# Output stores of a fused attention and feed-forward kernel: from SyncE's queue to ScalarE's, with a new plan of the order

## The chip, the cores and the metric

The kernel runs on one core of one Trainium2 chip. The metric is the device time in microseconds of one execution. TensorE (PE), VectorE (DVE), ScalarE (ACT) and GpSimd (POOL) compute; SyncE (SP) only issues DMAs. ACT and POOL have queues of their own in which DMAs can be issued too.

## The reference

Eight batches of eight heads, 576 queries each, head size 64. The keys of a batch are 16 beacons, which every query sees, and 576 causal keys. The outputs of all heads make a matrix x of 4608 tokens by 512, which goes through a gated feed-forward layer of width 1536. Cut to what matters:

```python
k_all = np.concatenate([beacon_k, k], axis=2)          # (8, 8, 592, 64)
v_all = np.concatenate([beacon_v, v], axis=2)
scores = np.matmul(q, k_all.transpose(0, 1, 3, 2)) / np.sqrt(64)
scores = np.where(causal, -1e9, scores)                # beacons never masked
a = np.exp(scores - scores.max(-1, keepdims=True))
a /= a.sum(-1, keepdims=True) + 1e-09
attn = np.matmul(a, v_all)                             # (8, 8, 576, 64)
x = attn.transpose(0, 2, 1, 3).reshape(4608, 512)
out = (np.maximum(x @ w_gate, 0) * (x @ w_val)) @ w_out
```

Inputs and the output are float32; the matmuls run in bfloat16.

## The kernel before

**Stages.** For every batch q, k and v are loaded in pieces of 128 partitions by 512 elements into eight staging tiles `st` (the helper `staged`, loads at L557 to L657), rounded to bfloat16 tiles `h` or `v` (L518, L471, mostly on POOL), and q and k are turned by TensorE against an identity (L529) and copied out of PSUM into `qT` and `kT` (the helper `copy`, L467 on ACT, L469 on DVE). In batch 7 the turning is done by a DMA transpose (L574). Scores are made in steps of 64 by 64 tiles (L756) into PSUM banks; DVE adds the mask and finds the row's extreme (L704), ACT takes the exponential with its sum (L711), DVE the reciprocal (L717), POOL multiplies the probabilities by it (L722). A DMA transpose issued by SP turns the probabilities, `pb` to `pTb` (L842; in the first batch TensorE does it, L832). The products with v (L852, L875) are copied into `xT`, the feed-forward input, which holds all tokens transposed.

**Feed-forward.** The function `ffn` works on ten spans of tokens (`SPANS`, 240 to 512 wide). For each of 12 slices of the width there are four gate matmuls (L913), a relu out of PSUM by ACT into a tile `g` (L924), four value matmuls (L918), and a product by DVE into `hT` (L929). Then, for every 128 tokens of the span, 12 output matmuls (L944) fill a PSUM bank; ACT or DVE copies it into one of three tiles `osb` (L954), and a DMA stores it (L958). The feed-forward work of early tokens runs between the attention work of later batches. All its PSUM comes from a share of at most three banks (`F_MOST`); scores have at most five (`SC_MOST`), out of eight in all.

**What sets the order.** The order is not written by hand. Every piece of work is a task given to `Plan.add` with its engine (or several to choose from), a cost, what it depends on, the buffers that it holds, and a priority. `Plan.order` (L190) then makes a list schedule: at each step it takes the task that can start first, then by lateness and priority, and books its cost on its engine. SP's queue is one such engine, called DMA; tasks of DMA carry a pair, the time for the issue and the time on the wire. The order that comes out is what each engine's queue gets, and engines work through their queues strictly in that order. While TensorE has nothing to do in the plan's first 160 us, filler matmuls (L996) are put in.

**Names that the change touches.** `BEHIND` (L44) makes the load at a place in a batch's list wait until a quad of another batch has been normalised, by a small memset on POOL that holds the staging tile. `W0` (L55) is the time in the plan before which no weight load (`weight`, L479, issued by POOL at L481) is placed. `PACE` (L66) times the batch number (and a half for its second quad) is the time before which no scores of it are placed (L978). A store is one task of DMA (L961) behind its copy (L960):

```python
q_ = nc.scalar if c else nc.sync
ev = add("ACT" if c else ("ACT", "DVE"), {"ACT": c_act(w), "DVE": c_dve(w)}, evict, (prev,), (ps[c], osb[c]), -1000 + prio)
add("DMA", (0.4, 0.78 / halves), store, (ev,), (osb[c],), prio + OUT)
```

`c` is 1 only for the second half of the very last 64 tokens, which are split in two columns of 256; that one store is issued by ACT, the other 37 by SP.

Of the kernel before, what the change touches and what calls it, by code (L numbers as in the profile page):

```python
# [20 lines left out]
RANK1 = -14.0  # L21
# [12 lines left out]
NEXT = -0.5  # L34
ON_PE = 2
TURN = (7,)
TURN_FIRST = 100
TURN_LOAD = 1.5
BIGSTEP = 2
# [1 line left out]
ENG = [("POOL", "DVE"), ("POOL",), ("POOL",)]  # L41
F_MOST = 3
HELD = {(1, 0): ("v", 0, 0), (1, 2): ("g", 0, 1024), (1, 4): ("v", 0, 1024)}
BEHIND = {(2, 2): (1, 0), (2, 7): (1, 1)}  # L44
MARK = 0.08
AB_FIRST = 0
W_FIRST = 0
# [4 lines left out]
ORDER0 = ("k00", "q00", "K", "Q", "k10", "q10", "v", "v", "k01", "q01", "k11", "q11", "v", "v", "v")  # L52
W_COLS = [(0, 512), (512, 512), (1024, 512)]
W_ROWS = 4
W0 = 14.0  # L55
W_STEP = 1.4
W_ISSUE = 0.85
W_MOVE = 0.72
# [4 lines left out]
SPANS = [240, 336, 512, 512, 512, 512, 512, 512, 512, 448]  # L63
FIRST_MOST = 3
AFTER = [[0.0, 12.0]]
PACE = 38.0  # L66


class Slots:
# [227 lines left out]
def kernel(  # L297
# [99 lines left out]
    def c_act(n):  # L397
        return 0.06 + 0.00083 * n
# [98 lines left out]
    def new_batch(b, prio, work):  # L497
# [54 lines left out]
        def load_pair(kind, p, prio):  # L552

            src, s0 = {"k": (k, 0), "q": (q, 64 - Nb)}[kind]
            st = staged()

            def fetch(_):  # L557
                if b in TURN:
                    for i in range(2):
                        nc.sync.dma_start(st.tile.rearrange("p (n h d) -> p h n d", h=2, d=D)[:, i],  # L560
                                          src[b, 4 * (p // 2) + p % 2 + 2 * i, s0:s0 + MAIN, :].rearrange("(n p) d -> p n d", p=P))
                    return
                nc.sync.dma_start(st.tile.rearrange("p (h e) -> p h e", h=2),
                                  src[b, bass.ds(4 * (p // 2) + p % 2, 2, step=2), s0:s0 + MAIN, :].rearrange("h (p j) d -> p h (j d)", j=4))

            ld = add("DMA", (1.0, TURN_LOAD) if b in TURN else (0.5, 0.87), fetch, (held,), (st,), prio[0])
            dst = t.kT if kind == "k" else t.q
            h16, ca = rounded(dst, st, P, neg_scale if kind == "q" else 1.0, prio, ld,
                              lambda to, src: [(to, src)] if b in TURN else [(
                to.rearrange("p (j h d) -> p h j d", h=2, j=4), src.rearrange("p (h j d) -> p h j d", h=2, j=4))])  # L570
            zeros = on_zeros.get(b) if kind == "q" else None
            c0 = Nb if kind == "k" else 64
            if b in TURN:
                t.rows[kind, p] = [add("DMA", (1.22, 0.177 * 4), lambda _: nc.sync.dma_start_transpose(  # L574
                    dst.tile[:, p, c0:c0 + MAIN].rearrange("p (j n) -> p j n", j=4), h16.tile), (ca, zeros), (h16, dst), prio[0] - TURN_FIRST)]
                return
            ps, tu = turned(h16, P, ca, prio)

            def evict(x):
                copy(x.engine, dst.tile[:, p, c0:c0 + MAIN].rearrange("p (n j) -> p n j", j=4),  # L580
                     ps.tile.rearrange("p (j n) -> p n j", j=4))

            t.rows[kind, p] = [add(("ACT", "DVE"), {"ACT": c_act(512), "DVE": c_dve(512)}, evict, (tu, zeros), (ps, dst), prio[1])]

        def load_half(kind, g, half, prio):

# [58 lines left out]
                                        evict, (tu, zeros), (ps, dst), prio[1])]  # L645

        def load_v(c, prio):
            st = staged()
            rows = min(P, SK - P * c)

            def fetch(_):
                s3 = st.tile.rearrange("p (h d) -> p h d", h=H)
                if c == 0:
                    nc.sync.dma_start(s3[:Nb], heads(beacon_v, b, 0, Nb))
                    nc.sync.dma_start(s3[Nb:], heads(v, b, 0, P - Nb))
                else:
                    nc.sync.dma_start(s3[:rows], heads(v, b, P * c - Nb, rows))  # L657

            ld = add("DMA", (1.1 if c == 0 else 0.55, V_MOVE * rows / P), fetch, (held,), (st,), prio[0])
            t.rows["v", c] = add(eng, cost, lambda x: copy(x.engine, t.v.tile[:rows, c, :], st.tile[:rows]),  # L660
                                 (ld,), (st, t.v), prio[1])

        at, held = 0, None
        for what in ORDER0 if b == 0 else "KQ0011v2233vvvv":
            pr = (prio + 0.01 * at, work + 0.01 * at)
            if what in "KQ":
# [238 lines left out]
    def ffn(m0, mt, deps, prio):  # L905
        hid, vals = [], []
        hT = [Hold(hid_s, 1 + (mt + P - 1) // P) for _ in range(NF)]
        for nf in range(NF):
            psg, psv, g = Hold(f_s, 2), Hold(f_s, 2), Hold(gate_s, 2)

            def gate(_, nf=nf, psg=psg):
                for ki in range(KM):
                    nc.tensor.matmul(psg.tile[:, :mt], wg_r[:, ki, nf * P:(nf + 1) * P], xT[:, ki, m0:m0 + mt],  # L913
                                     start=(ki == 0), stop=(ki == KM - 1))

            def val(_, nf=nf, psv=psv):
                for ki in range(KM):
                    nc.tensor.matmul(psv.tile[:, :mt], wv_r[:, ki, nf * P:(nf + 1) * P], xT[:, ki, m0:m0 + mt],  # L918
                                     start=(ki == 0), stop=(ki == KM - 1))

            n0 = nf * P // 512 * 512
            a = add("PE", 4 * c_pe(mt), gate, deps + vals[max(nf - 3, 0):max(nf - 2, 0)] + [weight_in["g", ki, n0] for ki in range(KM)], (psg,),
                    prio + 0.02 * nf)
            r = add("ACT", c_act(mt), lambda _, psg=psg, g=g: nc.scalar.activation(  # L924
                g.tile[:, :mt], psg.tile[:, :mt], AF.Relu), (a,), (psg, g), -1000 + prio)
            b_ = add("PE", 4 * c_pe(mt), val, [a] + [weight_in["v", ki, n0] for ki in range(KM)], (psv,),
                     prio + 0.02 * nf + 0.01)
            vals.append(b_)
            hid.append(add("DVE", c_dve(mt), lambda _, psv=psv, g=g, nf=nf: nc.vector.tensor_mul(  # L929
                hT[nf].tile[:, :mt], g.tile[:, :mt], psv.tile[:, :mt]), (r, b_), (psv, g, hT[nf]), -1000 + prio))  # L930
        prev = None
        for t0 in range(0, mt, P):
            rows = min(P, mt - t0)

            halves = 2 if rows <= 64 else 1
            w = DM // halves
            ps, osb = [Hold(f_s, 4 if halves == 1 else 2) for _ in range(halves)], [Hold(osb_s, 2) for _ in range(halves)]
            prev = prev if halves > 1 else None
            k = NF // 3 * (2 * halves - 1)
            for part in range(NF // k):  # L940
                def outp(_, part=part, t0=t0, rows=rows, ps=ps, w=w, halves=halves, k=k):
                    for nf in range(k * part, k * part + k):
                        for c in range(halves):
                            nc.tensor.matmul(ps[c].tile[64 * c:64 * c + rows, :w], hT[nf].tile[:, t0:t0 + rows],  # L944
                                             wo_r[:, nf, w * c:w * c + w], start=(nf == 0), stop=(nf == NF - 1))

                need = [prev] + hid[k * part:k * part + k] + [weight_in["o", nf, 0] for nf in range(k * part, k * part + k)]
                if part == 0:
                    need += hid[:11]
                prev = add("PE", k * c_pe(w) + SWITCH * (halves - 1), outp, need, tuple(ps) + tuple(hT[k * part:k * part + k]),  # L950
                           prio + 0.3 + 0.01 * part - (0.5 if part else 0))
            for c in range(halves):
                def evict(x, c=c, ps=ps[c], osb=osb[c], rows=rows, w=w):
                    copy(x.engine, osb.tile[64 * c:64 * c + rows, :w], ps.tile[64 * c:64 * c + rows, :w])  # L954

                def store(_, c=c, osb=osb[c], rows=rows, t0=t0, w=w):
                    q_ = nc.scalar if c else nc.sync
                    q_.dma_start(out[m0 + t0:m0 + t0 + rows, w * c:w * c + w], osb.tile[64 * c:64 * c + rows, :w])  # L958

                ev = add("ACT" if c else ("ACT", "DVE"), {"ACT": c_act(w), "DVE": c_dve(w)}, evict, (prev,), (ps[c], osb[c]), -1000 + prio)  # L960
                add("DMA", (0.4, 0.78 / halves), store, (ev,), (osb[c],), prio + OUT)  # L961


    T0 = 10.0
# [6 lines left out]
        weight("o", ko, W_ROWS, 0, DM, -15 + 0.3 * i, WWORK + 0.01 * i - (50 if i < W_FIRST else 0))  # L971
        i += 1
    for b in range(B):
        batches.append(new_batch(b, {0: -20, 1: RANK1}.get(b, b * T0 - 8), b * T0 - AHEAD if b else -20))
    for b in range(B):
        for i, vals in enumerate([("AB", "CDE")] if b >= SPLIT else [("AB",), ("CDE",)]):
            for g in range(2):
                quad(batches[b], g, vals, b * T0 + (4 * g if b >= SPLIT else 4 * i + 2 * g) - (AB_FIRST if b < SPLIT and i == 0 else 0), AFTER[b][i] if b < SPLIT else PACE * (b + g / 2))  # L978
        last(batches[b], b * T0 + 8)
    for t in batches:  # L980
        for held, (b, g) in t.late:
            for d in batches[b].normed[g]:
# [47 lines left out]
```

## Time and profile before

| | us |
|---|---|
| median of three runs | 403.38 |
| the three runs | 400.04, 403.38, 404.54 |
| the profiled execution's own time | 399.48 |
| its span, first to last instruction | 397.8 |
| last output matmul ends, about | 393.7 |

The profiled execution is one of its own, beside the three runs. In the rows of the views PE is TensorE's matmuls and PEld its weight loads, which run beside them; a q behind an engine's name (SPq, ACTq) is its queue's own work, such as issuing a DMA. A row of the waits gives the engine and line that waited, for whom, the time in total in microseconds, how many times, and the longest. A row of a timeline gives start and length in microseconds, the engine, the line, the operation, the tiles written and read, the shapes and the count of equal instructions. A row of a line's view gives counts and shortest, median and longest duration in nanoseconds. A row of the windows gives the stretch, its length, the busy time and count of each engine, the granted clock as a share, the DMA engines' share and GB/s.

### The profile page before, as it was taken

Reading aid. Unit: us, or ns where it says so; the run is one execution under the profiler, and the core shown is the slowest. Engines: PE = TensorE matmul, PEld = TensorE weight load, DVE = VectorE, ACT = ScalarE, POOL = GpSimd, SP = SyncE. Lnnn points to the kernel's source line nnn. Section 1 sums busy time; section 2 is a strip of 40 time slices with the busy share of each in tenths; the row PEclk is TensorE's granted clock in tenths of the full one; section 3 lists DMA queues with packets and bytes.
Section 4 is the critical chain, followed back from the end, with each engine's and each line's share of the span. In section 5 each row is a group of like instructions: output and inputs, shape, how many; then the busy total and the mean of one; then the engine's idle time right before and its main releaser. Section 6 shows DMA issues by size and latency. Waiting matters only on the chain.

```text
span 397.8 us, 9897 instructions
## 1 busy us (share of the span) xinstructions
PE 386.6 (97%) x3235; PEld 203.8 (51%) x3278; DVE 287.6 (72%) x1024; ACT 261.7 (66%) x820; POOL 234.2 (59%) x454
## 2 busy tenths in 40 slices
PE   6999999999999999999999999999999999999995
PEld 4667855655454545455455445444454544444543
DVE  3999899788988697879697969687758733342432
ACT  2999699868967788668877878587737721320320
POOL 6899979849977576869669848646653520000000
PEclk9999999999999999999999999999999999999999
DMA  7999989999999799989999989798979184001102
GB/s 183 233 205 226 250 154 180 214 232 256 247 209 204 197 224 221 176 227 263 189 166 298 208 146 183 164 221 184 196 138 234 25 127 145 2 0 57 50 1 93
DMA packets 184100, 68.87 MB, mean 173 GB/s; under 512 B 158384, under 2 KB 179504, under 8 KB 184048
## 3 DMA queue, kind: packets, MB, share of 16 engines
q1 hardware_dynamic: 179216, 63.46, 73.7%
q0 software_dynamic: 4752, 4.72, 7.5%
q8 instruction: 25, 0.41, 0.5%
q14 instruction: 27, 0.22, 0.2%
q10 hardware_dynamic: 80, 0.07, 0.1%
HBM read 38.54 MB, written 9.44 MB: 121 GB/s over the span
## 4 chain that ended last, share of the span: by engine, by line
PE 88%; POOL 3%; DVE 3%; DMA 2%; issue 1%; SPq 1%; ACT 0%; POOLq 0%; ACTq 0%
PE f L918 23%; PE f L944 23%; PE f L913 22%; PE f L756 7%; PE f L852 6%; PE f L529 3%; DMA st<-in_q_dram 2%; POOL xT L722 2%; DVE f L704 2%; PE f L832 1%; PE f L996 1%; PE f L875 1%; PE f L806 1%; DVE osb L469 1%; POOL h L518 1%
## 5 line engine op out<-in xcount | busy, mean ns | idle before, releaser
L722 POOL TENSOR_SCALAR pb<-pb,small 128x448 bf16<-128x448 bf16 (+8 forms) x272 | 141.5, 539 | 70.5 <-DVE small L717 69.8
L711 ACT ACTIVATE pb<-f,small 128x320 bf16<-128x320 f32 (+8 forms) x272 | 143.9, 553 | 22.6 <-DVE small L704 17.7
L704 DVE CUSTOM_DVE_ANT_0 f<-f,mask 128x576 f32<-128x576 f32 (+8 forms) x288 | 133.7, 515 | 14.3 <-PE f L756 9.1
L918 PE MATMUL f<-xT,wv_r 128*128 128x512 bf16 (+3 forms) x467 | 107.3, 358 | 0.7
L913 PE MATMUL f<-xT,wg_r 128*128 128x512 bf16 (+3 forms) x468 | 105.4, 357 | 0.6
L929 DVE TENSOR_TENSOR hT<-g,f 128x512 bf16<-128x512 f32 (+3 forms) x120 | 75.4, 631 | 37.3 <-PE f L918 32.1
L944 PE MATMUL f<-wo_r,hT 128*128 128x512 bf16 (+3 forms) x438 | 99.6, 374 | 1.3 <-issue 0.5
L924 ACT ACTIVATE g<-f 128x512 f32<-128x512 f32 (+3 forms) x120 | 66.3, 562 | 50.9 <-PE f L913 44.2
L913 PEld LDWEIGHTS <-wg_r 128*128 128x128 bf16 x480 | 45.3, 98 | 43.7 <-issue 1.2
L918 PEld LDWEIGHTS <-wv_r 128*128 128x128 bf16 x480 | 43.4, 98 | 44.5 <-issue 5.2
L944 PEld LDWEIGHTS <-hT 128*128 128x128 bf16 (+2 forms) x456 | 42.1, 100 | 46.3 <-issue 2.1
L711 ACT ACTIVATION_READ_ACCUMULATOR pb<-f,small 128x1 f32 x272 | 60.9, 224 | 0.0
L518 POOL TENSOR_SCALAR h<-st 128x512 bf16<-128x512 f32 (+1 forms) x93 | 49.0, 541 | 11.0 <-DMA st<-in_q_dram 6.9
L469 DVE COPY osb<-f 128x512 f32<-128x512 f32 (+2 forms) x32 | 21.7, 682 | 28.1 <-PE f L944 27.7
L704 DVE DVE_READ_ACCUMULATOR2_ANT small<- 128x1 f32 x296 | 41.6, 141 | 0.0
L467 ACT CAST xT<-f 128x240 bf16<-128x240 f32 (+2 forms) x56 | 21.2, 385 | 30.7 <-PE f L852 29.5
L756 PE MATMUL f<-kT,qT 64*64 64x512 bf16 (+7 forms) x640 | 34.4, 295 | 0.1
L717 DVE RECIPROCAL small<-small 128x1 f32<-128x1 f32 (+3 forms) x136 | 20.9, 161 | 13.5 <-ACT pb L711 9.8
L529 PE MATMUL f<-ident,h 128*128 128x128 bf16 (+1 forms) x288 | 26.8, 222 | 1.6 <-POOL h L518 1.4
L529 PEld LDWEIGHTS <-h 128*128 128x128 bf16 (+1 forms) x288 | 20.0, 101 | 14.6 <-POOL h L518 4.0
L852 PE MATMUL f<-pTb,v 128*64 128x320 bf16 (+3 forms) x488 | 26.7, 253 | 0.0
L471 POOL TENSOR_SCALAR v<-st 128x512 bf16<-128x512 f32 (+1 forms) x38 | 23.2, 617 | 4.0 <-DMA st<-in_v_dram 4.0
(61 smaller groups left out, 217.5 us busy)
## 6 DMA issues: line engine op xcount, KB each, us to landing
out_dram<-osb SPq DMA_DIRECT2D x34, 256.0 KB, 2.4
st<-in_k_dram SPq DMA_DIRECT2D x28, 256.0 KB, 5.0
st<-in_q_dram SPq DMA_DIRECT2D x28, 256.0 KB, 5.1
st<-in_v_dram SPq DMA_DIRECT2D x24, 256.0 KB, 5.6
st<-in_k_dram SPq DMA_DIRECT2D x16, 128.0 KB, 4.2
st<-in_q_dram SPq DMA_DIRECT2D x16, 128.0 KB, 3.1
st<-in_v_dram SPq DMA_DIRECT2D x8, 224.0 KB, 5.2
wg_r<-in_moe_w_gate_dram POOLq DMA_DIRECT2D x3, 512.0 KB, 7.3
```

What stands on the lines that cost most here:

```text
L518: (nc.gpsimd if x.engine == "POOL" else nc.vector).tensor_scalar(to, src, by, 1.0, ALU.mult, ALU.mult)
L529: nc.tensor.matmul(to, h16.tile[:rows, a * P:(a + 1) * P], ident[:rows, :rows], start=True, stop=True)
L704: nc.vector.tensor_tensor_reduce(out=view(i, n - m), in0=view(i, n - m), in1=msk, scale=1.0, scalar=at(7) if m < n else 3.0e38, op0=ALU.ad ...
L711: nc.scalar.activation(ph.tile.rearrange("p a n -> p (a n)")[:, a:a + n], view(i), AF.Exp, bias=at(i), scale=-1.0, accum_out=at(4 + i))
L722: nc.gpsimd.tensor_scalar(one, one, at(8 + i), 1.0, ALU.mult, ALU.mult)
L756: nc.tensor.matmul(banks[k][b_].tile[64 * i:64 * i + 64, off:off + n], t.q.tile[r, 2 * g + i, 64 * j:64 * j + 64], t.kT.tile[r, 2 * g + i, ...
L852: nc.tensor.matmul(ps.tile[64 * hh:64 * hh + 64, d0:d0 + w], t.v.tile[:rows, c, D * h:D * h + D], rhs(64 * hh), start=(c == 0), stop=(c == ...
L913: nc.tensor.matmul(psg.tile[:, :mt], wg_r[:, ki, nf * P:(nf + 1) * P], xT[:, ki, m0:m0 + mt], start=(ki == 0), stop=(ki == KM - 1))
L918: nc.tensor.matmul(psv.tile[:, :mt], wv_r[:, ki, nf * P:(nf + 1) * P], xT[:, ki, m0:m0 + mt], start=(ki == 0), stop=(ki == KM - 1))
L924: r = add("ACT", c_act(mt), lambda _, psg=psg, g=g: nc.scalar.activation(g.tile[:, :mt], psg.tile[:, :mt], AF.Relu), (a,), (psg, g), -1000 ...
L929: hid.append(add("DVE", c_dve(mt), lambda _, psv=psv, g=g, nf=nf: nc.vector.tensor_mul(hT[nf].tile[:, :mt], g.tile[:, :mt], psv.tile[:, :m ...
L944: nc.tensor.matmul(ps[c].tile[64 * c:64 * c + rows, :w], hT[nf].tile[:, t0:t0 + rows], wo_r[:, nf, w * c:w * c + w], start=(nf == 0), stop ...
```

## The change

All stores are issued by ACT. In the plan a store is a task of ACT with a cost of 0.12, and its time on the wire is kept as before. A copy out of PSUM may still be made by ACT or DVE; the store behind it is ACT's in both cases. The order is planned anew with other constants: `BEHIND` loses one of its two entries, `W0` goes from 14.0 to 15.7, `PACE` from 38 to 36, and two lists by batch come in, `STEPS_AT` (added to the time before which scores are placed) and `LASTS` (in place of the constant 8 in the priority of a batch's last rows). `LOADS`, `RANKS` and `LAZIES` are lists of zeros.

```diff
-BEHIND = {(2, 2): (1, 0), (2, 7): (1, 1)}
+BEHIND = {(2, 7): (1, 1)}
...
-W0 = 14.0
+W0 = 15.7
...
-PACE = 38.0
+PACE = 36.0
+LOADS = [0, 0, 0, 0, 0, 0, 0, 0]
+STEPS_AT = [0, -6, 6, -6, 0, 0, 0, 0]
+RANKS = [0, 0, 0, 0, 0, 0, 0, 0]
+LASTS = [8, 8, 8, 16, 8, 4, 8, 8]
+LAZIES = [0, 0, 0, 0, 0, 0, 0, 0]
+VCAST = 9
+STORES = 1
...
+            if b >= QUADS:
...
+            if b >= VCAST:
...
-                    q_ = nc.scalar if c else nc.sync
+                    q_ = nc.scalar if c or STORES else nc.sync
                     q_.dma_start(out[m0 + t0:m0 + t0 + rows, w * c:w * c + w], osb.tile[64 * c:64 * c + rows, :w])
...
-                add("DMA", (0.4, 0.78 / halves), store, (ev,), (osb[c],), prio + OUT)
+                add(*(("ACT", 0.12) if STORES else ("DMA", (0.4, 0.78 / halves))), store, (ev,), (osb[c],), prio + OUT, move=0.78 / halves if STORES else 0.0)
...
-        batches.append(new_batch(b, {0: -20, 1: RANK1}.get(b, b * T0 - 8), b * T0 - AHEAD if b else -20))
+        batches.append(new_batch(b, {0: -20, 1: RANK1}.get(b, b * T0 - 8 + LOADS[b]), b * T0 - AHEAD if b else -20))
...
-                quad(batches[b], g, vals, b * T0 + (4 * g if b >= SPLIT else 4 * i + 2 * g) - (AB_FIRST if b < SPLIT and i == 0 else 0), AFTER[b][i] if b < SPLIT else PACE * (b + g / 2))
-        last(batches[b], b * T0 + 8)
+                quad(batches[b], g, vals, b * T0 + RANKS[b] + (4 * g if b >= SPLIT else 4 * i + 2 * g) - (AB_FIRST if b < SPLIT and i == 0 else 0), AFTER[b][i] if b < SPLIT else PACE * (b + g / 2) + STEPS_AT[b])
+        last(batches[b], b * T0 + LASTS[b])
```

The two branches for `QUADS = 9` and `VCAST = 9` (another way to turn q and k in pairs, and v loads with a cast issued by POOL) are entered for batches numbered 9 and above; there are batches 0 to 7.

More of the change, by code (lines that the diff above doesn't have):

```diff
@@ L36 @@
 TURN = (7,)
+QUADS = 9
+TLAZY = 0.0
 TURN_FIRST = 100
@@ L576, in load_pair @@
                 return
+            if b >= QUADS:
+                t.rows[kind, p] = []
+                waiting.append((kind, dst, h16, ca, zeros))
+                if len(waiting) == 2:
+                    turned_pair(p, c0, prio)
+                return
             ps, tu = turned(h16, P, ca, prio)
@@ L583, in load_pair, with turned_pair, turn, evict @@
             t.rows[kind, p] = [add(("ACT", "DVE"), {"ACT": c_act(512), "DVE": c_dve(512)}, evict, (tu, zeros), (ps, dst), prio[1])]
+        def turned_pair(p, _, prio):
+            todo, waiting[:] = list(waiting), []
+            ps = [Hold(v_ps, 3) for _ in range(2)]
+            ps[0].next, ps[1].prev = ps[1], ps[0]
+            def turn(_):
+                for x, (_, _, h16, _, _) in enumerate(todo):
+                    for j in range(4):
+                        for r in range(2):
+                            for c in range(2):
+                                rows = slice(64 * r, 64 * r + 64)
+                                nc.tensor.matmul(ps[r].tile[64 * c:64 * c + 64, 256 * x + 64 * j:256 * x + 64 * j + 64],
+                                                 h16.tile[rows, j * P + 64 * c:j * P + 64 * c + 64], ident[rows, rows],
+                                                 start=True, stop=True)
+            tu = add("PE", 0.24, turn, [x[3] for x in todo] + [on_ident], (*[x[2] for x in todo], *ps), prio[1],
+                     part=2, lazy=TLAZY + LAZIES[b])
+            for x, (kind, dst, _, _, zeros) in enumerate(todo):
+                def evict(e, x=x, kind=kind, dst=dst):
+                    at = 512 * next(j for j, y in enumerate(bank) if y is ps[0].tile)
+                    c0 = Nb if kind == "k" else 64
+                    both = psum[:, at:at + 1024].rearrange("p (r y) -> p r y", r=2)[:, :, 256 * x:256 * x + 256]
+                    copy(e.engine, dst.tile[:, p, c0:c0 + MAIN].rearrange("p (r n j) -> p r n j", r=2, j=4),
+                         both.rearrange("p r (j n) -> p r n j", j=4))
+                t.rows[kind, p].append(add(("ACT", "DVE"), {"ACT": c_act(512), "DVE": c_dve(512)}, evict, (tu, zeros), (*ps, dst), prio[1]))
         def load_half(kind, g, half, prio):
@@ L647, in load_v, with take @@
         def load_v(c, prio):
+            rows = min(P, SK - P * c)
+            if b >= VCAST:
+                def take(_):
+                    v3 = t.v.tile[:, c].rearrange("p (h d) -> p h d", h=H)
+                    if c == 0:
+                        nc.gpsimd.dma_start(v3[:Nb], heads(beacon_v, b, 0, Nb))
+                        nc.gpsimd.dma_start(v3[Nb:], heads(v, b, 0, P - Nb))
+                    else:
+                        nc.gpsimd.dma_start(v3[:rows], heads(v, b, P * c - Nb, rows))
+                t.rows["v", c] = add("POOL", W_ISSUE * (2 if c == 0 else 1), take, (batches[-1].rows["v", NC - 1],), (t.v,), prio[1], 0.1, move=V_MOVE * rows / P)
+                return
             st = staged()
-            rows = min(P, SK - P * c)
             def fetch(_):
@@ L661, in load_v @@
                                  (ld,), (st, t.v), prio[1])
-        at, held = 0, None
+        at, held, waiting = 0, None, []
         for what in ORDER0 if b == 0 else "KQ0011v2233vvvv":
```

## The prediction

> **What bounds the kernel now.** I read the page first: the span, the busy shares, the clock line and the DMA line.
>
> ```profile
> span 397.8 us, 9897 instructions
> ...
> PE 386.6 (97%) x3235; PEld 203.8 (51%) x3278; DVE 287.6 (72%) x1024; ACT 261.7 (66%) x820; POOL 234.2 (59%) x454
> ...
> PE   6999999999999999999999999999999999999995
> ...
> PEclk9999999999999999999999999999999999999999
> DMA  7999989999999799989999989798979184001102
> ```
>
> TensorE works in every slice but the first and the last, at the full granted clock. Next comes the view by windows, cut at 66 us and at 330 us. The reason for 66: read instruction by instruction, both programs give TensorE the same order up to the instruction that starts at 66 us in the trace, and again over the last 833 of some 6,557. What the new plan can move on TensorE lies between.
>
> ```profile
> 0.00:66.00 66.00, 61.82 (x676) 42.19 (x678) 55.57 (x258) 52.81 (x168) 56.65 (x116) 1.00 1.02 204
> 66.00:330.00 264.00, 261.35 (x2219) 130.76 (x2254) 208.71 (x733) 194.14 (x626) 177.56 (x339) 1.00 0.95 198
> ```
>
> The columns are PE, PEld, DVE, ACT and POOL. In the middle stretch PE is idle for 264.00 - 261.35 = 2.65 us only. That is the first bound: whatever order the new plan finds, it can win little there. Busy PE can hide short waits, so I also read who made PE and its weight loads wait.
>
> ```profile
> PE f L996 <- POOL mask L415: 2.0, 1, 2.0
> PE f L529 <- POOL h L518: 1.4, 3, 0.8
> PE f L832 <- POOL xT L722: 0.6, 1, 0.6
> PE f L944 <- issue: 0.5, 3, 0.2
> ```
> ```profile
> PEld L756 <- issue: 17.4, 48, 0.4
> ...
> PEld L529 <- POOL h L518: 4.0, 8, 1.3
> ```
>
> Two things are to be seen. The large item, 17.4 us, is the price of changing to score matmuls (L756): 48 pauses of 0.36 us before a 64-row weight load, paid whatever the queues do. And the only engine that PE really runs into is POOL, with its casts (L518). ScalarE and SyncE, whose work this change shifts, stand in none of PE's rows. They wait themselves:
>
> ```profile
> ACT g L924 <- PE f L913: 44.2, 40, 11.3
> ```
> ```profile
> SPq L958 <- DVE osb L469: 71.8, 18, 27.0
> ```
>
> ACT waits for PE before its relu; SP stands for 71.8 us at stores whose data is not there yet, the longest 27.0 us in the last stretch, when nothing is behind it.
>
> **The change, part by part.** *Stores move from SP to ACT.* All 38 then stand in ACT's queue; 37 are new there. By the order of the new program 25 of them lie ahead of the last 48-matmul output phases, that is in the busy stretch, and 13 behind. Their price:
>
> ```profile
> L958 SPq DMA_DIRECT2D out_dram<-osb x37: 332/372/802, 59.9 to 394.2; - x37
> ```
> ```profile
> L958 ACTq DMA_DIRECT2D out_dram<-osb x1: 567/567/567, 394.1 to 394.1; - x1
> ```
> ```profile
> 393.71 0.42 DVE L469 COPY osb<-f 64x256 f32<-64x256 f32 x1 [0.73 <-PE f L944]
> 393.74 0.37 ACT L467 COPY osb<-f 64x256 f32<-64x256 f32 x1 [9.45 <-PE f L944]
> 394.14 0.57 ACTq L958 DMA_DIRECT2D out_dram<-osb  x1
> 394.15 0.57 SPq L958 DMA_DIRECT2D out_dram<-osb  x1
> ```
> ```profile
> L469 DVE COPY osb<-f 128x512 f32<-128x512 f32 (+2 forms) x32 | 21.7, 682 | 28.1 <-PE f L944 27.7
> ```
>
> One issue holds its queue for 0.33 to 0.57 us. The planner books 0.12 us for it (0.4 us on SP before), so ACT falls behind its plan by 0.21 to 0.45 us at each: 25 x 0.57 = 14.2 us of ACT's time at most, 25 x 0.33 = 8.3 us at least. To this comes a new wait: most stores (18 of the 25) follow a copy made by DVE, and ACT, which works in order, stands at the store until that copy is done. Between 0 and one copy, 0.68 us, each; I take 0.3 us, since ACT is placed there by the same plan that places the copy: 5.4 us. Queued behind the standing store are the relu (L924), which frees a PSUM bank for the next gate matmuls, and the exponentials (L711), which free the banks for the next scores. ACT's idle time in the stretch is 264.00 - 194.14 = 69.9 us; after the change 50 us are left, and ACT is then busy for some 214 us, as DVE is now (208.71). What of this reaches PE? At least nothing, as in the rows above, where ACT stands in none. At most all the issue time, 14.2 us. The nearest row is the one other engine that PE runs into, POOL, busy for 177.56 us in the stretch: 1.4 us on PE. I take +1.0 us.
>
> *SP is rid of its stores.* The 25 issues and their waits no longer stand ahead of loads and transposes. One place where that may matter is on the chain of waits:
>
> ```profile
> 137.15 5.42 DMA st<-in_q_dram
> ```
> ```profile
> 135.46 0.34 SPq L958 DMA_DIRECT2D out_dram<-osb  x1
> ...
> 137.15 0.54 SPq L563 DMA_DIRECT2D st<-in_q_dram  x1
> ```
> ```profile
> 143.41 0.40 PE L529 MATMUL f<-ident,h 128*128 128x128 bf16 x4 [0.17 <-POOL h L518]
> ```
>
> The load at 137.15 stood behind a store, POOL cast it late, and PE lost 0.17 us. All such losses together are at most PE's 1.4 us row on L518. Below that lies 0, if the loads come when they did; they can also collide earlier with transposes, which costs what it gains. I take -0.4 us.
>
> *The trade of queues brings no bandwidth.* The DMA line stands at 9 in most slices, and the bytes are the same. [...]
>
> *The order planned anew.* By the order of both programs the new plan has the same matmuls less one filler (87 for 88), and 66 blocks of scores for 65.
>
> ```profile
> L996 PE MATMUL f<-mask,ident x88: 272/273/421, 2.0 to 87.9; 128*128 128x256 bf16 x88
> ```
>
> One filler less is worth at most 0.27 us; I take -0.1. One more entry into scores costs 0.36 us by the row of 17.4; leaving them costs something too: +0.4 (bounds 0 and 0.8). Casts and copies keep their numbers per engine nearly: DVE copies 30 output tiles for 32 and more of xT, ACT the rest.
>
> *W0 from 14 to 15.7.* On POOL the first weight load moves behind four of the six norms that now follow it:
>
> ```profile
> 14.66 0.94 POOL L481 DMA_DIRECT2D wg_r<-in_moe_w_gate_dram  x1
> 15.64 2.84 POOL L722 TENSOR_SCALAR xT<-xT,small 128x128 bf16<-128x128 bf16 x6
> ```
> ```profile
> wg_r<-in_moe_w_gate_dram POOLq DMA_DIRECT2D x3, 512.0 KB, 7.3
> ```
> ```profile
> 26.31 0.38 PE L913 MATMUL f<-xT,wg_r 128*128 128x240 bf16 x2
> ```
>
> Four norms are 4 x 0.47 = 1.9 us. The weights land about 14.66 + 7.3 = 22.0 now and 23.9 then, 2.4 us before their first matmul. That cover gone, each microsecond later is one on PE. The last of the six norms still stand behind the load, so nothing is won. Cost 0. PACE, STEPS_AT, LASTS and the removed BEHIND entry act through the order alone, which is priced above; the new branches for QUADS and VCAST are not entered, as no batch is numbered 9.
>
> *The end.* The last two stores, now side by side, follow each other on ACT: 394.14 + 2 x 0.33 + 0.05 = 394.85 for 394.72 now; +0.1 us (bounds 0 and 0.6).
>
> The sum against the profiled execution: 399.48 (its span 397.8 and 1.7 around it) + 1.0 - 0.4 - 0.1 + 0.4 + 0.1 = 400.5, so +1.0 us. That execution is below the median of the runs, 403.38 (400.04 to 404.54); the four readings together average 401.9. Fresh runs will scatter likewise, so I put the forecast at 401.9 + 1.0, about 402.9 us.
>
> **The rivals.** *ACT's stores stuck behind SP's transposes (slower).* SP spends long on each transpose of a probability tile:
>
> ```profile
> L842 SPq DMA_TRANSPOSE pTb<-pb x28: 3728/4218/5842, 63.6 to 324.9; - x28
> ```
>
> 28 x 4.2 = 118 us of the 265 us from 63.6 to 328.7, or 45%. [...] Four 512-column matmuls fill the next bank meanwhile (0.86 us by this chain row),
>
> ```profile
> 99.11 1.73 PE f L913 x8
> ```
>
> so PE loses up to 11 x 1.2 = 13 us: 407 to 416 us, 411 in the middle. It decides if ACT's issue rows reach over 1 us. [...] For it: no transpose ever met an ACT issue in this trace. [...] By that rule the time would be this rival's; chance 0.17.
>
> *ACT waits at the head of its queue for DVE's copies (slower).* DVE is the busier engine; where it runs late, ACT stands 0.68 us and issues for 0.57: 1.25 us, 0.39 more than a bank covers, 18 times: +7 us, 408 to 410. Against it: DVE's copies wait for PE, 27.7 of their 28.1 us, so they come at once. Chance 0.12.
>
> *Loads in time (faster).* If the runs at 403 and 404 us lose their time to loads standing behind stores, all runs come down to the best one less the 1.4 us: 398 to 399. For it: the chain at 137 us. Against it: 0.17 us is what PE lost there. Chance 0.16. That the change does not do what it says is excluded by the order of the program.
>
> **How the numbers follow.** About 1%, 4 us, is what a measurement of this kernel can tell, given its runs. The forecast has 0.55, with its own range from 399.5 to 406: 0.02 of it faster by over 1%, 0.48 within, 0.05 slower. Transposes: 0.17 slower. Head of the queue: 0.09 slower, 0.03 within. Loads in time: 0.11 faster, 0.05 within. Together 0.13, 0.56 and 0.31. The range takes in most of the loads' case below and the head-of-queue case above, 398.5 to 409.5; beyond it lie the larger half of the transposes' case and the tails.
>
> **What would show it.** Right: PE's idle time between 66 and 330 us still under 4 us, ACT in none of PE's rows with more than 1.5 us, ACTq L958 rows at 0.33 to 0.6 us, ACT's wait for DVE osb under 10 us. Wrong by the first rival: ACTq L958 maxima of 2 us and more, at the times of L842. By the second: a row of ACTq waiting for DVE osb above 15 us in the busy stretch and PE waiting for ACT. By the third: the L529 rows on POOL gone and runs that no longer scatter. A new stall of PE on V products (L852) for a late transpose would upset all of it.

## The result and the profile after

The changed kernel takes 405.43 us (median of 22 runs, 401.86 to 409.30); the kernel before, run beside it on the same chip, takes 401.0 us (median of 22 runs, 398.95 to 404.54). The ratio is 1.0089 with a 95% interval of 1.0063 to 1.0115: slower by 0.9%. The ratio compares the faster runs alone, without the four slowest of the changed kernel (408.12 us and more); the median of the other 18 is 404.03 us. The profiled execution took 401.86 us with a span of 400.2 us.

The page of the changed kernel, in the lines that were read of the kernel before:

```profile
span 400.2 us, 9921 instructions
...
PE 388.9 (97%) x3277; PEld 203.1 (51%) x3277; DVE 286.2 (72%) x1024; ACT 264.3 (66%) x820; POOL 233.6 (58%) x453
...
PE   6899999999999999999999999899999999999995
```

A slice is 10.0 us. TensorE now has one below 9 in the middle, the 26th, at 250 to 260 us. The waits of PE name who was late:

```profile
PE f L538 <- POOL h L527: 1.7, 2, 1.1
PE f L997 <- ACT pb L764: 1.4, 1, 1.4
PE f L538 <- DVE h L527: 0.6, 1, 0.6
PE f L538 <- DVE small L757: 0.4, 1, 0.4
```

ScalarE stood in none of these rows before. Now output matmuls (L997, before L944) waited once, for 1.4 us, for an exponential (L764, before L711). Why the exponential was late stands in ScalarE's own waits, and the view of one line gives what the store itself cost:

```profile
ACT pb L764 <- DMA st<-in_v_dram: 3.9, 1, 3.9
...
ACT xT L476 <- DMA st<-in_k_dram: 1.6, 1, 1.6
```
```profile
L1011 ACTq DMA_DIRECT2D out_dram<-osb x38: 338/338/608, 59.4 to 397.2; - x38
```

One store holds ScalarE for 0.34 us in the median and 0.61 at most. Three were issued while one of SyncE's transposes of probabilities was running (137.01, 182.20 and 303.27 us; these transposes took 3.8 to 5.5 us), and took 0.34 us each too. But ScalarE waited 3.9 us for a *load of V*, though an exponential reads no loaded buffer. The chain of waits around that place (the first columns are start and length in us) shows what lay between:

```profile
253.64 3.42 DMA st<-in_v_dram
257.06 0.02 issue
257.08 0.02 ACTq L1011
257.10 0.04 issue
257.14 0.34 ACTq L1011
257.48 0.05 issue
257.52 0.79 ACT pb L764 x2
```

The load was issued at 253.64 us and landed at 257.06; at 257.14 ScalarE issued a *store*, and at 257.52 it went on. ScalarE's last work before had ended at 253.60. So the store waited 3.5 us for the landing of a load that it has nothing to do with. The instructions and the traces of the runs show how: in each of the eleven traces, the 232 DMAs that SyncE and ScalarE issue name eight semaphores, 29 DMAs each, taken in turn in the program's order, and none of the 224 that follow another on its semaphore, eight places behind it, starts before that one has landed, whichever engine issued it. In the kernel before, such waits fell on SyncE, with only other DMAs behind them: in its trace five DMAs of SyncE start 0.06 to 0.07 us behind such a landing, the one at 214.45 us after the longest stand, 0.53 us.

Eight stores of the changed kernel, in two groups of four, lie in bursts of loads. These three of them stood for a landing, worked out from the trace (times in us; the DMA named is the one eight places earlier; "stood" counts up to the issue):

| store issued | ScalarE free since | DMA eight places before | landed | stood |
|---|---|---|---|---|
| 216.80 | 216.08 | st<-in_k_dram | 216.72 | 0.7 |
| 257.14 | 253.60 | st<-in_v_dram | 257.06 | 3.5 |
| 259.49 | 258.30 | st<-in_k_dram | 259.41 | 1.2 |

Each starts 0.08 us behind the landing.

### The profile page after: what moved, and what is told of

Its sections match the earlier page's. It is cut to its first block, busy times and chain, and to the rows that moved or that the text cites. A ratio compares the mean times of both kernels' runs of the same rounds, so it can differ in the third digit from the quotient of the medians.

```text
span 400.2 us, 9921 instructions
## 1 busy us (share of the span) xinstructions
PE 388.9 (97%) x3277; PEld 203.1 (51%) x3277; DVE 286.2 (72%) x1024; ACT 264.3 (66%) x820; POOL 233.6 (58%) x453
## 4 chain that ended last, share of the span: by engine, by line
PE 79%; POOL 6%; DMA 5%; DVE 3%; SPq 2%; issue 2%; ACT 1%; ACTq 0%; POOLq 0%; DVEq 0%
PE f L971 22%; PE f L966 22%; PE f L997 19%; PE f L809 6%; PE f L905 5%; PE f L538 3%; DMA st<-in_k_dram 3%; POOL pb L775 3%; DVE f L757 2%; POOL xT L775 2%; ACT pb L764 1%; PE f L885 1%; DMA st<-in_beacon_k_dram 1%; POOL h L527 1%; DMA st<-in_v_dram 1%
## 5 line engine op out<-in xcount | busy, mean ns | idle before, releaser
L764 ACT ACTIVATE pb<-f,small 128x448 bf16<-128x448 f32 (+8 forms) x272 | 144.0, 550 | 24.2 <-DVE small L757 14.4
L757 DVE CUSTOM_DVE_ANT_0 f<-f,mask 128x64 f32<-128x64 f32 (+8 forms) x288 | 133.9, 514 | 10.8 <-PE f L809 5.6
L997 PE MATMUL f<-wo_r,hT 128*128 128x512 bf16 (+2 forms) x456 | 102.6, 374 | 1.4 <-ACT pb L764 1.4
L997 PEld LDWEIGHTS <-hT 128*128 128x128 bf16 (+2 forms) x456 | 41.7, 100 | 47.7 <-issue 4.3
L764 ACT ACTIVATION_READ_ACCUMULATOR pb<-f,small 128x1 f32 x272 | 59.9, 220 | 0.0
L478 DVE COPY osb<-f 128x512 f32<-128x512 f32 (+2 forms) x30 | 20.4, 680 | 25.0 <-PE f L997 24.7
L809 PE MATMUL f<-kT,qT 64*64 64x64 bf16 (+7 forms) x640 | 35.1, 293 | 0.6 <-DVE hT L982 0.3
L476 ACT CAST xT<-f 128x240 bf16<-128x240 f32 (+1 forms) x48 | 18.4, 392 | 25.1 <-PE f L905 23.4
L770 DVE RECIPROCAL small<-small 128x2 f32<-128x2 f32 (+3 forms) x136 | 20.8, 161 | 16.7 <-ACT pb L764 15.0
L809 PEld LDWEIGHTS <-qT 64*64 64x64 bf16 x640 | 14.4, 105 | 23.8 <-issue 19.6
```

Source lines behind the costliest of these rows:

```text
L757: nc.vector.tensor_tensor_reduce(out=view(i, n - m), in0=view(i, n - m), in1=msk, scale=1.0, scalar=at(7) if m < n else 3.0e38, op0=ALU.ad ...
L764: nc.scalar.activation(ph.tile.rearrange("p a n -> p (a n)")[:, a:a + n], view(i), AF.Exp, bias=at(i), scale=-1.0, accum_out=at(4 + i))
L809: nc.tensor.matmul(banks[k][b_].tile[64 * i:64 * i + 64, off:off + n], t.q.tile[r, 2 * g + i, 64 * j:64 * j + 64], t.kT.tile[r, 2 * g + i, ...
```

## The experiments

Theories of the loss: *shared semaphores* (ScalarE stands for landings of SyncE's loads, as above); *issue time* (25 times 0.34 us); *copy waits* (ScalarE stands for VectorE's copy); *order* (the new plan is worse by itself); and, against the first, *own queue* (anything else that a store costs where ScalarE issues it). Medians in us; ratios to the kernel before, run beside each on the same chip.

| run | order of | stores by | added on ScalarE | median | ratio, 95% interval |
|---|---|---|---|---|---|
| a_on_sp | after | SyncE | | 399.27 | 0.9971 (0.9942 to 1.0000) |
| a_dummy | after | SyncE | copies in the stores' places | 399.15 | 0.9980 (0.9960 to 1.0001) |
| b_dummy | before | SyncE | the same | 400.45 | 1.0023 (0.9994 to 1.0052) |
| b_on_act | before | ScalarE | | 404.36 | 1.0086 (1.0050 to 1.0121) |
| a_eight_sp | after | ScalarE, 8 by SyncE | | 400.74 | 1.0001 (0.9970 to 1.0031) |
| a_eight_act | after | SyncE, 8 by ScalarE | | 406.15 | 1.0139 (1.0092 to 1.0186) |
| a_waits | after | SyncE | copies, and 8 waits for landings | 406.01 | 1.0127 (1.0084 to 1.0171) |
| after_again | after | ScalarE | | 406.55 | 1.0151 (1.0104 to 1.0197) |
| a_on_sp_again | after | SyncE | | 399.42 | 0.9965 (0.9939 to 0.9992) |

**a_on_sp**: the order alone.

```diff
-                    q_ = nc.scalar if c or STORES else nc.sync
+                    q_ = nc.scalar if c else nc.sync
```

> The changed kernel with its order of work on TensorE, VectorE, ScalarE and GpSimd kept exactly, but its stores go back to SyncE (the last half stores stay with ScalarE as in the kernel before). Four theories of the 0.9% by which the changed kernel is slower. Shared semaphores: a store on ScalarE first waits until the DMA eight places before it in the program has landed, because both took the same completion semaphore, and such a wait on SyncE costs nothing; expected 1.000 to 1.004 of the kernel before (401 to 402.5 us). Issue time: 25 stores of 0.34 us on ScalarE in the busy stretch; expected the same 1.000 to 1.004. Copy waits: a store on ScalarE waits for VectorE's copy; the same again. Order: the new plan is worse by itself, whoever issues the stores; expected 1.007 to 1.011 (404 to 405.5 us). In the trace, by the first three, the two or three stalls of TensorE on ScalarE at 256 to 262 us (1.6 us together with their shadow on VectorE) are gone.

The plan still books the store on ScalarE, so TensorE, VectorE and GpSimd keep the order of the changed kernel. At 0.9971 the loss is gone, and the order is no worse than the old one but a little better: the theory of the order falls. The stretch from 66 to 330 us, first in the changed kernel, then here (PE's busy time is the third number):

```profile
66.00:330.00 264.00, 261.48 (x2240) 129.50 (x2238) 205.70 (x727) 196.24 (x624) 176.71 (x338) 1.00 0.92 192
```
```profile
66.00:330.00 264.00, 263.61 (x2255) 130.85 (x2253) 207.66 (x732) 196.60 (x626) 177.62 (x339) 1.00 0.95 196
```

PE is idle for 0.39 us here and for 2.52 us there: 2.1 of the 3.1 us between the two spans (400.2 and 397.1) are idle time of PE in this stretch. And the row of PE waiting for ScalarE is gone:

```profile
PE f L1049 <- POOL mask L424: 2.0, 1, 2.0
PE f L538 <- POOL h L527: 1.0, 1, 1.0
PE f L885 <- POOL xT L775: 0.6, 1, 0.6
PE f L809 <- DVE hT L982: 0.3, 1, 0.3
```

**a_dummy** and **b_dummy**: ScalarE's time and its wait for VectorE's copy, without a DMA. The first starts from a_on_sp, the second from the kernel before.

```diff
+                    if not c:
+                        nc.scalar.copy(idle[64 * c:64 * c + rows], osb.tile[64 * c:64 * c + rows, :IDLE])
                     q_ = nc.scalar if c else nc.sync
```

> As the run before it (the changed kernel's order, stores by SyncE), with a copy of 200 columns of the store's own buffer into a spare tile put on ScalarE exactly where the changed kernel has the store. So ScalarE pays about the store's 0.3 us each and waits for VectorE's copy as the store does, but for no landing. The copies write a spare tile that nothing reads. Shared semaphores: within 0.25% (1 us) of the run before it. Issue time or copy waits: as the changed kernel, 0.6 to 0.9% (2.5 to 3.6 us) over the run before it. Order: no difference to the run before it, and both at 1.009.

> The kernel before, its order and its stores on SyncE kept, with the same added copies of 200 columns on ScalarE behind each copy out of PSUM that a SyncE store follows (spare tile, nothing reads it). Shared semaphores and order: within 0.25% of the kernel before (400 to 402 us). Issue time or copy waits: 0.6 to 0.9% slower (403.5 to 404.5 us).

```profile
L1013 ACT CAST idle<-osb x37: 346/358/388, 60.2 to 394.7; 128x200 bf16<-128x200 f32 x34, 112x200 bf16<-112x200 f32 x1, 80x200 bf16<-80x200 f32 x1, 64x200 bf16<-64x200 f32 x1
```

The copies took 0.36 us each in a_dummy, a little more than the 0.34 us of a store, and read the same buffer. They cost nothing there that shows (0.9980 beside 0.9971), and 0.2% by the middle value in the order of before, 0.5% at the upper end of the interval. Issue time and copy waits together do not make the loss.

**b_on_act**: the old order, stores by ScalarE.

```diff
-                    q_ = nc.scalar if c else nc.sync
+                    q_ = nc.scalar
```

> The kernel before with its order kept, all stores issued by ScalarE where SyncE issued them in the plan. Shared semaphores: slower by 0.4 to 1% (402.5 to 405 us), and the trace shows at least two stores in the busy stretch that start within 0.15 us of the landing of the DMA eight places before them while ScalarE had been free for over 0.5 us. Issue time or copy waits: slower by 0.6 to 0.9%, without such starts. Order: within 0.25% of the kernel before.

Slower by 0.9%, as the change was, without the change's order or constants. In its trace five stores of the busy stretch stood for over 0.5 us and started 0.02 to 0.08 us behind the landing of the DMA eight places before: at 90.28, 137.87, 175.82, 181.40 and 218.53 us, the last after 1.65 us. Not all of this one execution's loss is the stores': its span is 403.3 us, and by the weight loads at common points of TensorE's program 2.2 us of it were lost ahead of 66 us, where the clock fell before any store had been issued (last section).

**a_eight_sp** and **a_eight_act**: only the stores that stand. The eight are the two groups of four at 213 to 224 and 257 to 265 us; the first kernel gives these alone back to SyncE, the second leaves these alone with ScalarE. The DMAs keep their places in the program.

```diff
-                    q_ = nc.scalar if c or STORES else nc.sync
+                    q_ = nc.scalar if c or next(count) not in CLOSE else nc.sync
```
```diff
+                    q_ = nc.scalar if c or next(count) in CLOSE else nc.sync
```

> The changed kernel with 8 of its 33 full-width stores given back to SyncE: the two groups of four at 213 to 224 us and 257 to 265 us, in the middle of bursts of loads, where the trace shows ScalarE standing until a load has landed (0.71, 3.5 and 1.19 us). The other 25 full stores, 17 of them in the busy stretch, stay with ScalarE. Its place in the plan and every store's place among the DMAs are as in the changed kernel. Shared semaphores: the loss goes, 0.997 to 1.001 of the kernel before. Own queue (every store costs the same where ScalarE issues it, by its queue or by taking transfers from the loads, some 4.5 us over 25 stores): 17 of 25 parts of the loss stay, 1.004 to 1.006.

> The counterpart: the changed kernel's order with all full-width stores on SyncE except these 8, which ScalarE issues. Shared semaphores: most of the loss is there, 1.003 to 1.009 of the kernel before, and PE's stall at 256 to 258 us is back. Own queue: 8 of 25 parts of the loss, 0.999 to 1.001.

Eight stores carry the whole loss: alone with ScalarE they give 1.0139, above what was expected, and between the 1.0089 and the 1.0151 of the changed kernel's two measurements, with intervals that overlap. The other 30, of which 17 lie in the busy stretch, show little of it: 1.0001, 0.3% over a_on_sp by the middle values, with intervals that overlap. (The 33 full-width stores and the other 25 of the first expectation are miscounted; ScalarE issues 38 in the changed kernel and 30 here.) A cost that every store pays alike would have left 1.004 to 1.006. The stall of TensorE is back in a_eight_act, where the store of the second group stood for 4.9 us (260.56; ScalarE free since 255.62, landing 260.49):

```profile
PE f L1000 <- ACT pb L765: 2.8, 1, 2.8
```

In this trace one issue of a store also took 2.23 us itself, at 216.38 us, beside issues of V loads by SyncE (the first row merges four of them; its 5.65 us run from the first to the last and hold pauses). ScalarE is not the cause of such a long issue: in a_on_sp the longest issue of a store by SyncE, at 215.67 us, took 2.45 us (third row).

```profile
215.53 5.65 SPq L711 DMA_DIRECT2D st<-in_v_dram  x4
...
216.38 2.23 ACTq L1014 DMA_DIRECT2D out_dram<-osb  x1
```
```profile
L1011 SPq DMA_DIRECT2D out_dram<-osb x37: 332/362/2447, 59.8 to 394.0; - x37
```

**a_waits**: the wait alone. As a_dummy, and at the eight places ScalarE also reads one element of the buffer into which the DMA that the changed kernel's store stood for loads. ScalarE issues none of these stores.

```diff
+                        at = LANDED.get(t.store)
+                        if at is not None:
+                            one = loads[at]
+                            while len(one.shape) > 2:
+                                one = one[:, 0]
+                            row = Nb if at in SECOND else 0
+                            nc.scalar.copy(idle[:1, :1], one[row:row + 1, :1])
```

(`loads` lists the loads in SyncE's order, and `LANDED` gives for each of the eight stores the load eight places before it. The order of work on each engine is that of a_dummy, but for one store on SyncE that comes one place later.)

> The changed kernel's order, all full-width stores on SyncE, the added copies of 200 columns on ScalarE at the stores' places as in the run named a_dummy; at the same 8 places ScalarE also copies one element of the staging buffer that is filled by the very load for which the changed kernel's store stood there. So ScalarE issues no store but stands for the same landings. Both kinds of copy write a spare tile that nothing reads. Shared semaphores: the wait alone makes the loss, 1.003 to 1.009 of the kernel before. Own queue, or anything else about a DMA issued by ScalarE: as a_dummy, 0.996 to 1.000.

The wait makes the loss by itself: 1.0127, where a_dummy had 0.9980. In the timeline ScalarE sits idle for 6.10 us until it may read the element, and TensorE 4.08 us for the exponential behind it:

```profile
259.68 0.19 ACT L1030 CAST idle<-st 1x1 bf16<-1x1 f32 x1 [6.10 <-issue]
259.90 0.69 ACT L774 ACTIVATE pb<-f,small 128x512 bf16<-128x512 f32 x1
...
260.73 5.28 PE L1009 MATMUL f<-wo_r,hT 128*128 128x512 bf16 x12 [4.08 <-ACT pb L774]
```

The load landed at 259.61 us, 2.6 us later than in the changed kernel, and of the eight reads only this one made ScalarE wait in this trace. So the run shows that such a wait is enough for a loss of this size, not what the changed kernel's shorter wait costs. The loss is more than was expected, because the stall has a sequel. The windows of this run, PE first and the granted clock behind POOL's count:

```profile
256.00:260.00 4.00, 0.64 (x3) 0.20 (x2) 0.00 (x0) 0.29 (x2) 0.00 (x0) 0.92 0.82 204
260.00:264.00 4.00, 3.27 (x8) 1.14 (x8) 2.48 (x9) 2.75 (x9) 2.85 (x5) 0.50 0.85 204
264.00:268.00 4.00, 4.00 (x28) 1.49 (x27) 1.47 (x8) 2.43 (x9) 2.77 (x5) 0.73 0.48 131
268.00:272.00 4.00, 4.00 (x20) 1.80 (x19) 3.24 (x13) 3.39 (x13) 1.35 (x3) 1.00 0.67 152
```

Cut finer, the granted clock is 0.50 from 259.32 to 266.15 us, and the twelve output matmuls take 5.28 us.

**after_again** and **a_on_sp_again**: the changed kernel traced a second time, and the faster version beside it.

> The changed kernel once more, for a second trace and on the same chip as the next run. Shared semaphores: 1.006 to 1.012 of the kernel before, and in the trace the stores at about 215 to 265 us again start within 0.15 us of the landing of the DMA eight places before them while ScalarE has been free; where TensorE's idle stretch at 256 to 262 us is over 2.5 us long, the granted clock falls below 0.9 in the 4 us after it, as in the runs a_eight_act and a_waits, and the time is over 406 us; where it is under 2 us, the clock stays at 1.00 and the time is under 404.5 us.

> The changed kernel's order with its stores on SyncE once more, since its interval touched 1. By every theory that holds the order to be sound: 0.994 to 0.999 of the kernel before, mean granted clock at or above 0.998 in nearly every run; beside the run before it, 0.986 to 0.991 of the changed kernel.

The changed kernel's ratio, 1.0151, lies above what was expected. In its second trace the store at this place stood for 4.4 us (258.45; ScalarE free since 254.04, landing 258.37), PE's idle time grew to 2.31 us, and the clock fell there too. The same twelve matmuls in the first trace, then in the second, with the windows of the second:

```profile
258.35 2.75 PE L997 MATMUL f<-wo_r,hT 128*128 128x512 bf16 x12 [1.44 <-ACT pb L764]
```
```profile
259.66 4.44 PE L997 MATMUL f<-wo_r,hT 128*128 128x512 bf16 x12 [2.31 <-ACT pb L764]
```
```profile
258.00:262.00 4.00, 2.34 (x7) 0.93 (x7) 2.33 (x8) 1.60 (x5) 2.08 (x4) 0.76 0.96 225
262.00:266.00 4.00, 4.00 (x30) 1.53 (x28) 1.72 (x10) 2.93 (x9) 2.60 (x5) 0.82 0.81 229
```

So 0.9 us more of idle time cost 1.7 us more of matmul time. The 2.31 us lie between the two cases of the expectation (over 2.5 us and under 2 us): the clock fell as in the first, and the time, 404.37 us, was that of the second. The changed kernel's order with its stores on SyncE was again a little faster than the kernel before, now with an interval that leaves 1 out (0.9965, up to 0.9992), and its median lies 1.8% below the changed kernel's on that chip (399.42 / 406.55 = 0.982).

## Why the prediction was wrong

The forecast was 402.9 us, within 1% of before; measured were 405.43 us and 0.9% more than before, at the edge of "within 1%", and over it in the second measurement.

- **Where it failed**: in "Stores move from SP to ACT", the step "To this comes a new wait", which listed one wait for a store, VectorE's copy. A store has a second one, for the DMA eight places before it. From that followed "I take +1.0 us" for what reaches PE. The sign was right; by the runs the term is the difference between the changed kernel and a_on_sp, 406.55 - 399.42 = 7.1 us on one chip, 3.1 us between the two spans of the first traces. It lies within the bounds of 0 to 14.2 us, but by luck and not for the reason that set them: a_dummy and b_dummy put the issue time and the copy wait, which the step priced at 8.3 to 14.2 and 5.4 us of ScalarE's time, at 0 to 0.2% of the whole. That the three stores of the table stood for 5.4 us together, the very sum that the step had for the copy waits, is chance.
- **Issue time per store** was put at 0.33 to 0.57 us; it was 0.34 in the median. That ScalarE's slack (69.9 us idle) would take it was right.
- **The order planned anew** (-0.1 and +0.4 us, so +0.3): a_on_sp has the new order with the stores still on SyncE, and so measures the order alone: 0.9971 and 0.9965, some 1.2 to 1.4 us faster. Small as was forecast, but wrong in sign.
- **SP rid of its stores** (-0.4 us): no run has this by itself. PE's row on POOL's casts, which was to shrink from 1.4 us, stands at 1.7 us and, in the second trace, 2.5 us; a_eight_sp, where SyncE is rid of 29 stores, is no faster than a_on_sp. No gain shows.
- **W0 at no cost, the end at +0.1 us**: no wait of PE for the weights stands in the rows after, and from the first common weight load of the last part (315.32 us before, 317.78 after) to TensorE's last one both programs take 77.98 us. Behind the last matmul the last store landed after 3.09 us, 2.75 before: 0.3 us for the 0.1 forecast, within its bounds. The 0.57 us that each of the two stores at 394 us took, issued side by side, is about what they took in the changed kernel one behind the other on ScalarE, at 396.61 and 397.24 us: 0.54 and 0.55 us.
- **PE's idle time of 2.65 us before**, the first bound, was read too literally: the trace of before has 3,235 matmuls for 3,278 weight loads, so 43 are not recorded and their time counts as idle. The traces with 3,277 for 3,277 can be compared, and a_on_sp has 0.39 us there.
- **From 399.48 to 401.9 us**: the readings were averaged to 401.9 us; fresh runs of before had medians of 400.0 to 401.0. Without this step, 1 to 2 us too high, the point would have been lower still.
- **Rival "stuck behind SP's transposes"** (411 us): refuted for the changed kernel, as the three stores issued inside a running transpose took 0.34 us each, and no store of its trace took over 0.61 us. The term 11 x 1.2 us was the author's estimate: 45% of the 25 stores, each waiting for half of a transpose of 4.2 us, less the 0.86 us of four matmuls into the next bank; no run shows it. The 3.5 us that the store at 257.14 us stood are in no row of ACTq, but in the gap ahead of its row of 0.34 us. Elsewhere single issues were longer: of two stores inside one transpose in b_on_act the first took 0.34 us and the second, at 232.63 us, 1.24 us, and the 2.23 us in a_eight_act lie beside loads; what made them long is open.
- **Rival "ACT waits at the head of its queue for DVE's copies"**: right that ScalarE stands at the head of its queue with exponentials behind it, wrong in whom it waits for (a_dummy).
- **Rival "Loads in time"** (398 to 399 us): nearly the time of a_on_sp, where SyncE still has the stores; so the stores' leaving is not what gains it.
- Of the signs that were to show the forecast right, the idle time under 4 us (2.52), the issue rows and PE's rows for ScalarE (1.4 at most) were met in the first trace, although the kernel was slower; in the second trace ScalarE's row is 2.3 us. The signs were set too wide for a loss of 3 us.

Left open: what the other 17 stores of the busy stretch cost, between nothing and 0.3% by the middle values; and whether the eight alone cost more than all do, which the intervals do not decide.

## What to carry to other kernels

When a DMA is moved to another engine's queue, list every semaphore on which the moved instruction waits, not only its data: a wait for an unrelated transfer cost nothing that showed here on SyncE, which only issues DMAs (0.9971 and 0.9965 with the stores there), and on ScalarE, which computes, it stopped the exponentials behind it, for 3.5 us at 257 us in the first trace of the changed kernel and 4.4 us at 258 us in the second. In a trace, look for issues that start a few hundredths of a microsecond behind some landing (0.02 to 0.08 us here) while their engine had long been free. A move of this kind is best tried first with the order kept (issuer alone) and then with the issuer kept (order alone); here the second was a small gain that the first had buried.

## What the hardware showed unexpectedly

TensorE's granted clock fell after pauses of 2.31 and 4.08 us in an otherwise full kernel, and not after one of 1.44 us. After 1.44 us of idle time (first trace of the changed kernel) the twelve matmuls behind it took 2.75 us at a granted clock of 1.00; after 2.31 us (after_again), 4.44 us; after 4.08 us (a_waits), 5.28 us. In the last two cases the clock fell to the same 0.50. The 0.76 and 0.82 above are means of windows that each hold a part of the fall: in after_again the clock was 0.50 from 260.05 to 263.46 us, for 3.41 us, and in a_waits for 6.83 us, twice as long. So the wait of 2.31 us was paid nearly twice: 2.31 us of idle time and 1.69 us of longer matmuls (4.44 for 2.75 us). How long a pause has to be for the clock to fall is not shown.

The old order has such a fall of its own now and then: in the trace of b_on_act, whose order is that of before, the window from 25 to 30 us, ahead of the first store, stands at 0.66 (0.50 from 26.51 to 29.92 us), though no pause of TensorE from 20 us to that fall was longer than 0.61 us.

```profile
25.00:30.00 5.00, 4.35 (x33) 2.82 (x33) 3.31 (x15) 3.57 (x12) 4.91 (x8) 0.66 1.23 203
```

In the 24 timed runs of a_on_sp and its repeat the mean granted clock was never below 0.998; of the 32 runs of the kernel before beside the first of them, 7 were below 0.997 and took 402.0 us and more. Without the runs below 0.997 the mean of the new order lies 0.3 us under that of before on each of the two chips (399.57 for 399.90 us, 399.56 for 399.91 us); with them it is 0.9 and 1.4 us. So the larger part of the new order's 0.3% goes with these falls; why the new order is free of them was not tried.
